# One-core MLP gradient kernel: from a fused forward and backward loop to four whole phases, with on-chip transposes and a deferred gelu derivative

## The chip, the cores and the metric

The kernel runs on one core of one Trainium2 chip. Its time is the device time of one execution in microseconds (us), measured on the chip; several executions are taken. An execution in the slow state shows a lower granted TensorE clock and a longer time; only fast executions are compared here. The profile is one execution recorded by the hardware profiler. Its span, from the first to the last instruction, is about 2 us shorter than the time of the same execution.

The engines are TensorE (PE in the profile, with its weight loads as PEld), VectorE (DVE), ScalarE (ACT), GpSimd (POOL) and SyncE (SP, which here only issues DMAs; SPq is its queue). PSUM is where matmuls accumulate; both kernels use eight 128 x 512 fp32 tiles of it.

## The reference

All arrays are bf16. S = 2048 rows, D = 448, F = 1792.

```python
h   = gelu_tanh(x @ w1 + b1)          # x: S x D, w1: D x F
out = h @ w2 + b2                     # w2: F x D
# and its gradients for a given grad_out g (S x D):
gw2 = h.T @ g                         # F x D
gh  = (g @ w2.T) * gelu'(x @ w1 + b1) # S x F
gx  = gh @ w1.T                       # S x D
gw1 = x.T @ gh                        # D x F
gb1, gb2 = gh.sum(0), g.sum(0)
```

There are six matrix products of the same size. D = 448 is three and a half times 128: where D is the contracted dimension (x @ w1 and g @ w2.T, called M1 and M4 below), the last 128-row tile is only half full.

## The kernel before

It works in blocks of 512 rows, on pairs of 128 columns of F (28 pairs in all). One loop does M1 and M4 of a pair and, between them, h @ w2 and gh @ w1.T of the block before. The half tile is padded with zero weights, so that M1 and M4 take four full matmuls per tile. In M1 one of the padding rows is not zero: it carries b1, against a row of ones in x, so that the bias costs no instruction. gelu' is computed at once from the z in PSUM. h and gh are stored to DRAM in transposed form and read back by transposing DMAs for gw2 and gw1.

```python
w1_sb = const.tile([P, KD, F], BF16, name="w1_sb")
nc.gpsimd.memset(w1_sb[0:DL, KD - 1, :], 0.0)          # 64 zero rows
...
for kt in range(KD):                                    # KD = 4
    mm_i = nc.tensor.matmul(ps1[:], lhsT=w1_sb[:, kt, fcols], rhs=xq[:, kt, :],
                            start=(kt == 0), stop=(kt == KD - 1))
nc.scalar.activation(out=hT_blk[:, ft, :], in_=ps1[:], func=ACT.Gelu_apprx_tanh)
sq_i = nc.scalar.activation(out=A[:, h, :], in_=ps1[:], func=ACT.Square, scale=...)
nc.vector.scalar_tensor_tensor(out=Bt[:, h, :], in0=A[:, h, :], ..., in1=ps1[:], ...)
...
pdma(nc.gpsimd, hT_dram_v[:, fts[0]:fts[1] + 1, scols], hT_blk[:, fts[0]:fts[1] + 1, :])
... # M4 of the pair, gh = (gelu') * ps4, store of ghT, then parts of h @ w2 and gh @ w1.T
# after the loop:
for ft in range(NF):                                    # gw2
    w_ts.append(nc.sync.dma_start_transpose(out=h_blk[:], in_=hT_dram[ft * P:(ft + 1) * P, :]))
    for st in range(NS):
        nc.tensor.matmul(ps_w[:, 0:D], lhsT=h_blk[:, st, :], rhs=g_all[:, st, :], ...)
... # gw1 in the same way from ghT_dram
```

## Time and profile before

The median is 301.95 us (three runs, 300.64 to 303.75).

| stage before | us | how read |
|---|---|---|
| start, to the first real matmul | 12.6 | timeline |
| fused loop | 194.3 | first matmul of the loop to first of gw2 |
| gw2 | 42.4 | to the first matmul of gw1 |
| gw1 and tail | 52.5 | to the end of the span |

From the page of the kernel before, its first two parts: busy time and share of each engine, and busy tenths in 40 equal slices of the span (PEclk is the granted TensorE clock in tenths).

```profile
span 301.8 us, 4020 instructions
PE 284.4 (94%) x1520; PEld 142.5 (47%) x1520; DVE 209.8 (70%) x317; ACT 147.6 (49%) x236; POOL 71.5 (24%) x89
PE   4589799999999999999999999999999999799994
PEclk9999999999999999999999999999999999799998
```

TensorE is busy almost throughout; what is left is the start and a dip near the end. The start in the timeline (start in us, duration, engine, line, operation, out<-in, and in brackets the idle time before it and what ended that):

```profile
9.85 0.28 POOL masks.py:199 TENSOR_SCALAR_AFFINE_SELECT ident<-ident 128x128 bf16<-128x128 bf16 x1 [7.39 <-DMA g_nat_108<-in_grad_out_dram]
10.18 0.48 PE L100 MATMUL ps_acc<-ident,x_nat_99 128*128 128x128 bf16 x3 [5.41 <-POOL ident masks.py:199]
12.56 1.86 PE L242 MATMUL ps_160<-xT_q,w_sb 128*128 128x512 bf16 x4 [0.52 <-DVE xT_q L106]
```

The transposes of x on TensorE need an identity matrix, whose second instruction on GpSimd runs only at 9.85 us. The dip near the end, in the chain of waits (start, duration, what the chain was in):

```profile
249.35 3.46 SPq L340
252.85 5.59 DMA gh_nat<-ghT_dram
258.57 5.30 PE ps_2370 L377 x16
263.87 3.45 PE ps_2388 L377 x16
```

The transposed reload of gh is late, TensorE pauses, and its next 16 matmuls take 5.30 us in place of 3.45. The last line also gives the pace of a 512-column matmul: 3.45 / 16 = 0.2156 us. For 448 columns the chain shows 3.03 us for 16, or 0.189.

The tail of gw1 is column-tiled (128*64), and its neighbours are not:

```profile
269.32 1.46 PE L377 MATMUL ps_2406<-gh_nat,x_all 128*128 128x512 bf16 x6
270.71 1.94 PE L383 MATMUL ps_2424<-gh_nat,x_all 128*64 128x256 bf16 x32
272.58 1.25 PE L377 MATMUL ps_2487<-gh_nat,x_all 128*128 128x512 bf16 x5
```

The change of tiling costs about 0.1 us on the way in and 0.1 us on the way out. And two activations of 512 columns follow each other on ScalarE every 0.48 us:

```profile
99.84 0.62 ACT L244 ACTIVATE hT_blk<-ps_1050 128x512 bf16<-128x512 f32 x1
100.32 0.63 ACT L245 ACTIVATE A<-ps_1050 128x512 f32<-128x512 f32 x1
```

### The profile page before, as it was taken

The page shows a single profiled execution, that of the slowest core. Times are in us where ns is not written, and L with a number is a line of the kernel's source. Part 1 is how long each engine was busy: PE and PEld are TensorE (multiplying, and loading weights), DVE is VectorE, ACT ScalarE, POOL GpSimd, SP SyncE. Part 2 cuts the span into 40 slices and gives each one's busy share as a digit, 9 for nine tenths or more (in the row PEclk, how much of TensorE's full clock was granted, in tenths as well). Part 3 has the DMA queues.
Part 4 walks back from the last instruction along what each step waited for, and adds up shares of the span by engine and source line. Part 5 has one row for each costly group of instructions (what it writes and reads, how often), then busy time and mean ns, then how long its engine had stood idle before and what let it go on. Part 6 is the DMA issues. An engine that isn't in the chain of part 4 may idle for free.

```text
span 301.8 us, 4020 instructions
## 1 busy us (share of the span) xinstructions
PE 284.4 (94%) x1520; PEld 142.5 (47%) x1520; DVE 209.8 (70%) x317; ACT 147.6 (49%) x236; POOL 71.5 (24%) x89
## 2 busy tenths in 40 slices
PE   4589799999999999999999999999999999799994
PEld 1355344444444444444444444555555558245542
DVE  0258999999999999878999778605600027857760
ACT  1099987759695756677665576112121212021211
POOL 2451010821063200522212111000210001242252
PEclk9999999999999999999999999999999999799998
DMA  4673197720579945743212314095889899999861
GB/s 134 192 206 137 41 182 168 303 114 37 130 189 375 389 155 103 213 165 130 104 72 92 116 42 187 15 223 78 169 178 171 181 213 195 183 222 164 283 206 61
DMA packets 96761, 49.18 MB, mean 163 GB/s; under 512 B 78803, under 2 KB 92596, under 8 KB 96742
## 3 DMA queue, kind: packets, MB, share of 16 engines
q1 hardware_dynamic: 91188, 31.60, 46.9%
q0 software_dynamic: 5264, 17.06, 15.0%
q10 hardware_dynamic: 290, 0.27, 0.4%
q8 instruction: 12, 0.20, 0.3%
q14 instruction: 7, 0.06, 0.1%
HBM read 7.92 MB, written 21.57 MB: 98 GB/s over the span
## 4 chain that ended last, share of the span: by engine, by line
PE 43%; DVE 9%; SPq 5%; ACT 4%; DMA 2%; issue 1%; POOL 0%; POOLq 0%; DVEq 0%
PE ps_acc L191 6%; PE ps_acc L204 6%; SPq L340 4%; DVE Ep L250 2%; DVE ghT_blk L263 2%; DVE Bt L246 2%; DMA gh_nat<-ghT_dram 2%; PE ps_2370 L377 2%; ACT Bt L249 2%; ACT Ct L248 1%; DVE Ep L251 1%; PE ps_2487 L377 1%; PE ps_2605 L377 1%; PE ps_2641 L377 1%; PE ps_2623 L377 1%
## 5 line engine op out<-in xcount | busy, mean ns | idle before, releaser
L191 PE MATMUL ps_acc<-w_sb,hT_blk 128*128 128x448 bf16 x224 | 47.7, 353 | 0.2
L204 PE MATMUL ps_acc<-w1T_sb,ghT_blk 128*128 128x448 bf16 x224 | 45.6, 353 | 0.0
L250 DVE SCALAR_TENSOR_TENSOR Ep<-Bt,A 128x1024 bf16<-128x1024 f32 x28 | 34.3, 1224 | 12.0 <-ACT Bt L249 11.7
L248 ACT ACTIVATE Ct<-Bt 128x1024 bf16<-128x1024 f32 x28 | 30.2, 1079 | 25.3 <-DVE Bt L246 25.3
L261 PEld LDWEIGHTS <-w2T_sb 128*128 128x128 bf16 x224 | 21.8, 98 | 27.5 <-issue 3.4
L242 PEld LDWEIGHTS <-w_sb 128*128 128x128 bf16 x224 | 22.1, 99 | 25.2 <-issue 2.8
L215 POOL DMA_DIRECT2D ghT_dram<-ghT_blk x28 | 20.3, 726 | 56.4 <-DVE ghT_blk L263 56.3
L355 DVE TENSOR_TENSOR gb_acc<-gh_nat 128x512 f32<-128x512 bf16 x7 | 4.8, 692 | 39.9 <-DMA gh_nat<-ghT_dram 33.1
L191 PEld LDWEIGHTS <-hT_blk 128*128 128x128 bf16 x224 | 21.8, 98 | 22.6 <-ACT hT_blk L244 0.9
L204 PEld LDWEIGHTS <-ghT_blk 128*128 128x128 bf16 x224 | 21.9, 98 | 21.2
L319 PEld LDWEIGHTS <-h_blk 128*128 128x128 bf16 x224 | 21.9, 98 | 20.5
L215 POOL DMA_DIRECT2D hT_dram<-hT_blk x28 | 20.3, 727 | 45.7 <-ACT hT_blk L244 31.3
L249 ACT ACTIVATE Bt<-Ct 128x1024 f32<-128x1024 bf16 x28 | 30.1, 1075 | 0.3
L377 PEld LDWEIGHTS <-x_all 128*128 128x128 bf16 x192 | 19.0, 100 | 21.1 <-issue 5.0
L357 DVE TENSOR_TENSOR gb_acc<-gb_acc,gh_nat 128x512 f32<-128x512 f32 x42 | 28.6, 723 | 0.3
L363 POOL PARTITION_ALL_REDUCE gb_all<-gb_acc x7 | 14.8, 2108 | 58.9 <-DVE gb_acc L358 58.9
L251 DVE TENSOR_TENSOR Ep<-Ct,Ep 128x1024 bf16<-128x1024 bf16 x28 | 19.2, 687 | 0.3
L206 ACT CAST gx_blk<-ps_acc 128x448 bf16<-128x448 f32 x16 | 8.4, 527 | 20.1 <-PE ps_acc L204 20.1
L193 DVE TENSOR_TENSOR o_blk<-ps_acc,b_bc 128x448 bf16<-128x448 f32 x16 | 9.8, 620 | 3.8 <-PE ps_acc L191 3.8
L311 DVE TENSOR_TENSOR gsum<-gsum,g_all 128x448 f32<-128x448 f32 x14 | 8.7, 625 | 0.5
L177 ACT ACTIVATE w2T_sb<-ps_acc 128x512 bf16<-128x512 bf16 x14 | 8.5, 730 | 0.0
L106 DVE COPY xT_q<-ps_acc 128x512 bf16<-128x512 bf16 x4 | 1.7, 425 | 9.7 <-PE ps_acc L102 9.7
(492 smaller groups left out, 468.7 us busy)
## 6 DMA issues: line engine op xcount, KB each, us to landing
hT_dram<-hT_blk POOLq DMA_DIRECT2D x28, 256.0 KB, 3.0
ghT_dram<-ghT_blk POOLq DMA_DIRECT2D x28, 256.0 KB, 2.7
out_dram<-o_blk SPq DMA_DIRECT2D x4, 448.0 KB
x_all<-in_x_dram SPq DMA_DIRECT2D x1, 1792.0 KB, 14.5
g_all<-in_grad_out_dram SPq DMA_DIRECT2D x1, 1792.0 KB
out_dram<-gx_blk SPq DMA_DIRECT2D x4, 448.0 KB, 3.1
out_dram<-gw_all SPq DMA_DIRECT2D x2, 784.0 KB, 5.5
out_dram<-gw_all SPq DMA_DIRECT2D x3, 384.0 KB, 2.7
```

The costliest lines, as they stand in the source:

```text
L191: nc.tensor.matmul(ps_o[:, 0:D], lhsT=hT_blk[:, ft, j * P:(j + 1) * P], rhs=w2_sb[:, ft, :], start=(ft == 0), stop=(ft == NF - 1))
L204: nc.tensor.matmul(ps_x[:, 0:D], lhsT=ghT_blk[:, ft, j * P:(j + 1) * P], rhs=w1T_sb[:, ft, :], start=(ft == 0), stop=(ft == NF - 1))
L215: i = eng.dma_start(out=out, in_=in_)
L242: mm_i = nc.tensor.matmul(ps1[:], lhsT=w1_sb[:, kt, fcols], rhs=xq[:, kt, :], start=(kt == 0), stop=(kt == KD - 1))
L248: tanh_i = nc.scalar.activation(out=Ct[:], in_=Bt[:], func=ACT.Tanh, scale=1.0 / 3.0)
L249: nc.scalar.activation(out=Bt[:], in_=Ct[:], func=ACT.Square)
L250: nc.vector.scalar_tensor_tensor(out=Ep[:], in0=Bt[:], scalar=1.0, in1=A[:], op0=ALU.subtract, op1=ALU.mult)
L251: nc.vector.tensor_tensor(out=Ep[:], in0=Ct[:], in1=Ep[:], op=ALU.subtract)
L261: nc.tensor.matmul(ps4[:], lhsT=w2T_sb[:, kt, fcols], rhs=gq[:, kt, :], start=(kt == 0), stop=(kt == KD - 1))
L319: nc.tensor.matmul(ps_w[:, 0:D], lhsT=h_blk[:, st, :], rhs=g_all[:, st, :], start=(st == 0), stop=(st == NS - 1))
L357: nc.vector.tensor_tensor(out=acc[:], in0=acc[:], in1=gh_nat[:, 2 * k:2 * k + 2, :], op=ALU.add)
L377: nc.tensor.matmul(ps_w[:, 0:wpair], lhsT=x_all[:, st, kt * P:(kt + 1) * P], rhs=gh_pair[:, st, :], start=(st == 0), stop=(st == NS - 1))
```

## The change

The kernel becomes four phases: the whole forward, gw2, the whole backward, gw1. h and gh go from SBUF to SBUF through transposing DMAs and stay there, so the DRAM copies vanish. z is kept in SBUF (`Z`), and gelu' is computed from it later (`emit_E`), in place, at lower priority. Of the half tiles, two are paired: the two matmuls with 64 rows each use different row halves of the array at the same time, so a pair of tiles takes 7 matmul slots in place of 8. With the padding goes the row of b1: the bias becomes an operand of two activations (`b1c`). gb1 comes from the accumulator of the VectorE operation that makes gh.

The order of instructions on each engine is fixed at build time by a scheduler, from its estimate of durations and from the priorities that the program gives.

```diff
+    def pair_mms(pss, lhs, rhs, fts):
+        for h, ft in enumerate(fts):
+            fc = slice(ft * P, (ft + 1) * P)
+            for n, kt in enumerate((0, 1, 3) if h == 0 else (0, 1, 2)):
+                nc.tensor.matmul(pss[h], lhsT=lhs[:, kt, fc], rhs=rhs[:, kt, :], start=(n == 0), stop=False)
+        for h, ft in enumerate(fts):                      # the two half matmuls
+            fc = slice(ft * P, (ft + 1) * P)
+            kt, ps_ = (2, slice(0, DL)) if h == 0 else (3, slice(DL, P))
+            nc.tensor.matmul(pss[h], lhsT=lhs[ps_, kt, fc], rhs=rhs[ps_, kt, :], start=False, stop=True)
...
+    for i in range(14):                                   # warm-up, 8 before
+        nc.tensor.matmul(pw[:], lhsT=warm[:, 0:P], rhs=warm[:, 0:SB], start=True, stop=True)
...
+    def emit_E(b, c):                                     # gelu' from z: 3 on ScalarE, 7 on VectorE
+        zc = Z[b][:, 2 * c:2 * c + 2, :]
+        nc.scalar.activation(out=s[:], in_=zc, func=ACT.Square)
+        nc.vector.tensor_scalar(out=v[:], in0=s[:], scalar1=GELU_A, scalar2=1.0, op0=ALU.mult, op1=ALU.add)
+        nc.vector.tensor_tensor(out=v[:], in0=v[:], in1=zc, op=ALU.mult)
+        nc.scalar.activation(out=v[:], in_=v[:], func=ACT.Tanh, scale=GELU_C)
+        nc.scalar.activation(out=n[:], in_=v[:], func=ACT.Square)
...                                                       # five more on VectorE
+    for b in range(NB):                                   # forward
+        for c in range(NPAIR + 1):
+            if c < NPAIR:
+                with tc.high_priority():
+                    pair_mms([p[:] for p in pss], w1_sb, xq, fts)
+                    for h, ft in enumerate(fts):
+                        nc.scalar.activation(out=hT[:, h, :], in_=pss[h][:], func=ACT.Gelu_apprx_tanh, bias=b1c[:, ft:ft + 1])
+                        nc.scalar.activation(out=Z[b][:, ft, :], in_=pss[h][:], func=ACT.Identity, bias=b1c[:, ft:ft + 1])
+                    for h, ft in enumerate(fts):
+                        nc.sync.dma_start_transpose(out=h_nat[:, b * SPB:(b + 1) * SPB, ft * P:(ft + 1) * P], in_=hT[:, h, :])
+            if c > 0:
+                with tc.high_priority():
+                    chain_step(acc, prev, w2_sb, c - 1)   # out += h @ w2, 8 matmuls of 448 columns
+                emit_E(b, c - 1)
...
+    g_all = big.tile([P, NS, D], BF16, name="g_all", tag="nat_d")
+    nc.gpsimd.dma_start(out=g_all[:], in_=g2.rearrange("(st p) d -> p st d", p=P))
...                                                       # gw2 from h_nat and g_all; gb2 sums; x_all
+    for b in range(NB):                                   # backward
+                pair_mms([p[:] for p in pss], w2T_sb, gq, fts)
+                for h, ft in enumerate(fts):
+                    nc.vector.scalar_tensor_tensor(out=ghT[:, h, :], in0=Z[b][:, ft, :], scalar=1.0, in1=pss[h][:], op0=ALU.add, op1=ALU.mult,
+                                                   accum_out=gb1_p[:, b, ft:ft + 1])
...                                                       # transposes of gh, chain_step with w1T_sb, then gw1
-    (the fused loop, the stores to and reloads from hT_dram and ghT_dram, the gb1 sums)
```

## The prediction

> **What bounds the kernel now.** TensorE. The page's first part gives PE 284.4 of 301.8 us (94%). From the timeline: 512-column matmuls start every 0.2156 us (16 in 3.45 us), 448-column ones every 0.189 us (16 in 3.03 us). Stages, from the chain of waits and the timeline: first real matmul at 12.6 us; fused forward/backward loop to 206.9; gw2 to 249; gw1 to 297.3; tail 4.5 us. The loop's matmuls alone (448 x 0.2156 + 448 x 0.189) are 181 us of its 194. In gw1 the chain passes through 14 transposing loads of DRAM copies (2.2 to 3.5 us of queue time each); PE waits 2.2 us at 256.4, then runs at clock 0.51 from 258.6 to 262: about 4 us lost there.
>
> **Removed.**
> - An eighth of the two K=448 products (64 zero rows): 448 matmuls become seven eighths, 12.1 us.
> - 72 of 88 PE transposes: about 4.5 us with their waits on ScalarE.
> - DRAM round trip of h and gh: 14.7 MB out, 14.7 MB back; the gw1 stall, 4 us.
> - gb1 sums on VectorE (36 us, off the path).
> - Startup: the identity is ready only at 9.85 us and PE is at half clock (0.43 us per matmul) until 16 us. More warm-up matmuls and a lighter GpSimd queue should save 5 us.
>
> **Added.**
> - 56 entries into row-tiled half pairs and 56 exits. The Trainium skill ("TensorEngine Tiling (Array Packing)", Key Properties) says that changing tiling mode drains TensorE. The trace agrees for column tiles: entering at 270.7 and leaving at 272.6 cost about 0.1 us each beyond the 16 x 0.109 us of pairs. At 0.2 us per pair that is 11 us: I expect it to give back nearly all of the 12.1 us.
> - 112 small transposing DMAs on SP. A 128 KB one from DRAM takes 1.25 us of SP's queue (timeline); two per pair is 2.5 us against 3.2 us of PE. SP is close to binding, not binding, if an SBUF source costs the same.
> - ScalarE: gelu and copy 4 x 0.48 us per pair (starts in the timeline), below PE's 3.2; deferred gelu' 3 x 1.06 us per pair fills gaps and the 42 us of gw2. VectorE likewise.
>
> **Sum (estimates from these durations).** Start 8; forward 28 x (7 x 0.2156 + 0.2 + 8 x 0.189) = 90; gw2 42.4; backward 90; gw1 42.7 (4 x 48 x 0.189 plus two column-tiled tails of 3.2); tail 3; about 4 for late w1/w2 pieces at startup, block edges and phase edges. Total 280 us: 7% faster. The gain comes from startup, PE transposes and gw1's stall, hardly from the removed zero rows.
>
> **What the profile would show.** PE busy near 95% still; first real matmul near 8 us; a pair of M1 (7 matmul slots) about 1.7 us, not 1.51, with weight-load idle at each mode change; gw2 at 3.03 us per tile without DMA waits; hT transposes on SP at 1.2 to 1.4 us each, SP queue about 85% full in forward and backward; no idle before gh_nat in gw1; ScalarE and VectorE below PE in every stage; gelu' finished before the backward needs it.
>
> **What would make it wrong.** SBUF-to-SBUF transposes costing over 1.6 us each: SP then paces both loops (each 0.1 us more is about 5 us). Scheduling: a gelu' activation of 1.06 us ahead of a gelu delays PE, if ScalarE has no slack. Startup loads (3.9 MB) too slow for pairs 2 to 4. Row-tile switches costing nothing (270) or double (291). Clock throttling after any PE gap.
>
> Predicted 280 us, range 268 to 297; faster by over 2% 0.83, within 2% 0.11, slower 0.06.

## The result, and the profile after

The changed kernel takes 320.87 us (median of four runs, 320.47 to 322.65). The ratio to the kernel before is 1.0636, 95% interval 1.058 to 1.0693. Ratios here are from the fast runs of both kernels in the same rounds, and not quite the ratios of the medians. The record gives no check of this run's results; its variants a1, a2, a4 and a5 below passed theirs. It is 6.4% slower, where 7% faster was predicted.

The same parts of the page as above:

```profile
span 318.7 us, 3910 instructions
PE 288.4 (91%) x1408; PEld 125.9 (40%) x1408; DVE 156.8 (49%) x348; ACT 171.5 (54%) x244; POOL 19.3 (6%) x26
PE   7238999999999997999997399999999999999994
PEclk9659999999999999999999679999999999999999
```

TensorE has fewer matmuls than before and is busy for longer. There is a hole at the start and one in the middle. Stage by stage, by the first matmul of each in the timeline:

| stage | predicted | measured | difference |
|---|---|---|---|
| start, to the first M1 | 8 | 20.9 | +12.9 |
| forward | 90 | 106.8 | +16.8 |
| gw2 | 42.4 | 42.4 | 0 |
| backward, to the first matmul of gw1 | 90 | 101.5 | +11.5 |
| gw1 and tail | 45.7 | 47.2 | +1.5 |
| allowance for stalls | 4 | (in the above) | -4 |
| sum | 280 | 318.7 (span) | +38.7 |

So three stages failed and two came as predicted. The start, in the timeline:

```profile
1.31 1.29 POOL L197 DMA_DIRECT2D g_all<-in_grad_out_dram  x1 [0.37 <-issue]
12.87 0.28 POOL masks.py:199 TENSOR_SCALAR_AFFINE_SELECT ident<-ident 128x128 bf16<-128x128 bf16 x1 [10.27 <-issue]
13.20 1.86 PE L125 MATMUL acc<-ident,x_nat_102 128*128 128x128 bf16 x16 [6.18 <-POOL ident masks.py:199]
13.66 5.89 DVE L222 TENSOR_TENSOR gsum<-gsum,g_all 128x448 f32<-128x448 f32 x9
19.47 0.41 DVE L127 COPY xT_q<-acc 128x512 bf16<-128x512 bf16 x1
20.90 4.08 PE L71 MATMUL ps<-xT_q,w_sb 128*128 128x512 bf16 x12 [0.79 <-DVE b1c L132]
```

The load of `g_all` (1.8 MB), written in the program after forward, has no dependence on it, and the scheduler put it first on GpSimd. The identity follows at 12.87 us. Worse, the gb2 sums (gsum) became ready with that load and stand on VectorE ahead of the copies of x transposed, which therefore end 5 us later.

Busy time of the engines by stretch (the stretch and its length, then busy us and number of instructions of PE, PEld, DVE, ACT and POOL, the granted clock, the DMA share and GB/s): forward, the first 17 us of backward, the rest of backward.

```profile
20.90:127.70 106.80, 101.43 (x449) 39.08 (x450) 56.23 (x107) 102.91 (x152) 5.93 (x5) 0.99 0.51 106
170.10:187.20 17.10, 9.55 (x34) 2.93 (x33) 16.87 (x38) 10.15 (x12) 1.89 (x2) 0.71 0.56 147
187.20:271.50 84.30, 84.30 (x418) 36.14 (x418) 34.00 (x106) 6.13 (x14) 2.29 (x3) 1.00 0.53 110
```

In forward both TensorE (101.4 of 106.8) and ScalarE (102.9) look full, which leaves two suspects. At the start of backward VectorE is full and TensorE half idle, at clock 0.71. Later in backward VectorE and ScalarE have much time to spare. What fills VectorE there (Z_98 is z of block 0, Z_101 of block 3; L242 makes gh, L153 is part of gelu'):

```profile
175.55 0.68 DVE L242 SCALAR_TENSOR_TENSOR hT<-Z_98,ps 128x512 bf16<-128x512 bf16 x1
182.38 0.69 DVE L153 TENSOR_TENSOR y<-y,Z_101 128x1024 bf16<-128x1024 bf16 x1
182.99 0.68 DVE L242 SCALAR_TENSOR_TENSOR hT<-Z_98,ps 128x512 bf16<-128x512 bf16 x1
183.73 1.67 PE L138 MATMUL acc<-w1T_sb,hT 128*128 128x448 bf16 x4 [4.80 <-DVE hT L242]
```

Between the two gh operations of the first pair stand 14 gelu' operations, of which the line of 182.38 is the last, and TensorE waits 4.80 us.

What TensorE does in forward, and in backward, in the timeline:

```profile
119.69 0.92 PE L138 MATMUL acc<-w_sb,hT 128*128 128x448 bf16 x4
120.55 0.39 PE L75 MATMUL ps<-xT_q,w_sb 64*128 64x512 bf16 x1
120.86 0.93 PE L138 MATMUL acc<-w_sb,hT 128*128 128x448 bf16 x4
121.73 0.39 PE L75 MATMUL ps<-xT_q,w_sb 64*128 64x512 bf16 x1
122.05 0.55 PE L138 MATMUL acc<-w_sb,hT 128*128 128x448 bf16 x2
...
190.20 0.39 PE L75 MATMUL ps<-gT_q,w2T_sb 64*128 64x512 bf16 x2
190.52 1.69 PE L138 MATMUL acc<-w1T_sb,hT 128*128 128x448 bf16 x8
192.05 1.46 PE L71 MATMUL ps<-gT_q,w2T_sb 128*128 128x512 bf16 x6
193.44 0.39 PE L75 MATMUL ps<-gT_q,w2T_sb 64*128 64x512 bf16 x2
```

In backward the two halves (64*128) stand together in 27 of the 28 pairs and start 0.003 us apart; one pair takes 193.44 - 190.20 = 3.24 us. That is 6 x 0.2156 + 8 x 0.189 = 2.81, one slot of 0.2156 for both halves, and 0.21 for entering and leaving the row-tiled mode, as predicted. In forward M1 and the chain are both of high priority, and the scheduler mixed them: of the 56 halves only 12 overlap with a partner (six starts 0.003 us after another half); the others run alone, and the array enters and leaves the mode 39 times instead of 28.

The idle time of TensorE that other engines ended (in total, times, longest), the three longest:

```profile
PE acc L138 <- DVE hT L242: 7.5, 2, 4.8
PE acc L125 <- POOL ident masks.py:199: 6.2, 1, 6.2
PE acc L131 <- DVE xT_q L127: 4.9, 1, 4.9
```

And ScalarE in forward, to be held against the 0.48 us above:

```profile
50.22 0.84 ACT L181 ACTIVATE Z_99<-ps,b1c 128x512 bf16<-128x512 f32 x1
50.78 0.85 ACT L180 ACTIVATE hT<-ps,b1c 128x512 bf16<-128x512 f32 x1
51.35 0.85 ACT L181 ACTIVATE Z_99<-ps,b1c 128x512 bf16<-128x512 f32 x1
```

They follow each other every 0.57 us. The Trainium skill ("ScalarE: Activation LUTs", What ACT_TABLE_LOAD costs) says that each per-partition pointer operand adds about 93 ns to an activation. The new gelu has such a bias (`b1c`), the old one had none, and the trace agrees: 0.57 against 0.48.

### The profile page after: what moved, and what is told of

The parts are those of the page before. It is cut to its first block, busy times and chain, and to the rows that moved or that the text cites. A ratio compares the mean times of both kernels' runs of the same rounds, so it can differ in the third digit from the quotient of the medians.

```text
span 318.7 us, 3910 instructions
## 1 busy us (share of the span) xinstructions
PE 288.4 (91%) x1408; PEld 125.9 (40%) x1408; DVE 156.8 (49%) x348; ACT 171.5 (54%) x244; POOL 19.3 (6%) x26
## 4 chain that ended last, share of the span: by engine, by line
PE 63%; DVE 22%; ACT 9%; DMA 4%; issue 2%; DVEq 0%; POOL 0%; POOLq 0%; ACTq 0%
PE acc L138 23%; PE ps L71 20%; PE acc L276 11%; PE ps L75 6%; DMA g_all<-in_grad_out_dram 4%; DVE y L155 3%; DVE v L149 3%; DVE y L153 3%; ACT hT L180 3%; DVE v L148 2%; PE acc L284 2%; DVE gsum L222 2%; DVE n L154 2%; DVE y L152 2%; ACT Z_101 L181 1%
## 5 line engine op out<-in xcount | busy, mean ns | idle before, releaser
L138 PEld LDWEIGHTS <-hT 128*128 128x128 bf16 x448 | 38.7, 98 | 59.8 <-issue 14.1
L138 PE MATMUL acc<-w_sb,hT 128*128 128x448 bf16 x224 | 55.1, 354 | 3.5 <-ACT hT L180 2.4
L138 PE MATMUL acc<-w1T_sb,hT 128*128 128x448 bf16 x224 | 47.6, 358 | 7.5 <-DVE hT L242 7.5
L71 PE MATMUL ps<-xT_q,w_sb 128*128 128x512 bf16 x168 | 45.9, 388 | 2.6 <-DVE b1c L132 0.8
L212 PE MATMUL acc<-g_all,h_nat 128*128 128x448 bf16 x224 | 42.5, 352 | 0.0
L71 PE MATMUL ps<-gT_q,w2T_sb 128*128 128x512 bf16 x168 | 42.2, 387 | 0.0
L180 ACT ACTIVATE hT<-ps,b1c 128x512 bf16<-128x512 f32 x56 | 38.5, 734 | 3.9 <-PE ps L75 3.7
L276 PE MATMUL acc<-gh_nat,x_all 128*128 128x448 bf16 x192 | 36.7, 352 | 0.0
L150 ACT ACTIVATE v<-v 128x1024 bf16<-128x1024 bf16 x28 | 30.0, 1086 | 3.2 <-DVE v L149 3.2
L151 ACT ACTIVATE n<-v 128x1024 bf16<-128x1024 bf16 x28 | 30.2, 1091 | 0.2
L276 PEld LDWEIGHTS <-x_all 128*128 128x128 bf16 x192 | 18.6, 98 | 17.6 <-issue 0.4
L242 DVE SCALAR_TENSOR_TENSOR hT<-Z_99,ps 128x512 bf16<-128x512 bf16 x14 | 9.1, 686 | 13.5 <-PE ps L75 13.5
## 6 DMA issues: line engine op xcount, KB each, us to landing
g_all<-in_grad_out_dram POOLq DMA_DIRECT2D x1, 1792.0 KB, 11.7
```

Source lines behind the costliest of these rows:

```text
L71: nc.tensor.matmul(pss[h], lhsT=lhs[:, kt, fc], rhs=rhs[:, kt, :], start=(n == 0), stop=False)
L138: nc.tensor.matmul(acc[j][:, 0:D], lhsT=lhs[:, h, j * P:(j + 1) * P], rhs=w[:, ft, :], start=(ft == 0), stop=(ft == NF - 1))
L150: nc.scalar.activation(out=v[:], in_=v[:], func=ACT.Tanh, scale=GELU_C)
L151: nc.scalar.activation(out=n[:], in_=v[:], func=ACT.Square)
L180: nc.scalar.activation(out=hT[:, h, :], in_=pss[h][:], func=ACT.Gelu_apprx_tanh, bias=b1c[:, ft:ft + 1])
L212: nc.tensor.matmul(ps_w[:, 0:D], lhsT=h_nat[:, st, ft * P:(ft + 1) * P], rhs=g_all[:, st, :], start=(st == 0), stop=(st == NS - 1))
```

## The experiments

The theory after reading the traces: (1) the early `g_all` load spoils the start; (2) in forward, either TensorE's separated halves or ScalarE's gelu' activations set the pace, and the two had to be told apart; (3) at the start of backward VectorE works off the gelu' of later blocks before the gh that TensorE waits for. The rivals were that the work itself is too much for ScalarE and VectorE wherever it is put, and that the transposing DMAs pace the loops. Eleven runs were made, of ten kernels. All edits are against the changed kernel unless said otherwise. Every edit is scheduled anew, so the order changes elsewhere too; where that matters it is said. The stages of all of them, in us, by the first matmul of each stage:

| kernel | first M1 | forward | gw2 | backward | span |
|---|---|---|---|---|---|
| changed kernel | 20.9 | 106.8 | 42.4 | 101.5 | 318.7 |
| a1_gall_late | 12.5 | 111.3 | 42.6 | 105.7 | 319.2 |
| a2_fullK | 21.3 | 110.9 | 42.6 | 98.7 | 320.8 |
| a3_noE (wrong results) | 21.3 | 105.0 | 42.6 | 90.7 | 306.7 |
| a4_pinned | 20.8 | 99.4 | 42.6 | 106.7 | 316.6 |
| a5_bwdprio | 21.0 | 108.1 | 42.6 | 93.5 | 312.3 |
| a7, pinned and noE (wrong results) | 20.7 | 92.4 | 42.4 | 90.9 | 293.5 |
| c2_balanced | 12.1 | 96.0 | 42.6 | 95.2 | 293.1 |
| c3_xT | 5.6 | 101.8 | 42.6 | 95.2 | 292.3 |
| c5_later | 6.1 | 101.8 | 42.4 | 91.3 | 288.8 |
| c6_fullK | 6.4 | 98.7 | 42.4 | 91.0 | 285.6 |

### a1_gall_late: the load of g_all after block 1

```diff
-    nc.gpsimd.dma_start(out=g_all[:], in_=g2.rearrange(...))
+    g_i = nc.gpsimd.dma_start(out=g_all[:], in_=g2.rearrange(...))
+    tc.add_manual_dep(g_i.ins, late_after.ins.name, ORDER, reason="g_all after block 1")   # order only
```

> The load of g_all (1.8 MB) is ordered behind the output store of block 1; nothing else is changed. Theory: in the changed kernel the scheduler issued it at 1.3 us on GpSimd's queue, ahead of the identity's second instruction (ready only at 12.9 us), and its arrival let the gb2 sums run on VectorE ahead of the copies of x transposed (5 us). Then the first M1 moves from 20.9 us to 12 to 14 us and the total falls by 6 to 9 us, to about 313. Rival: the identity is late for a reason of its own (something GpSimd does between its two instructions that has no link with the load); then only the 5 us of the sums come back, M1 at about 16 us, total about 316.

Measured: 320.32 us, ratio 1.0554 (1.0493 to 1.0616). The first M1 moved to 12.5 us and the identity to 9.67 us, as the theory said, so the cause of the late start is shown. But the total hardly moved: in the profiles the spans are 319.2 and 318.7 us. (The ratio looks 0.8% better because the kernel before was slower in these rounds, 303.84 us.) The 8.4 us came back as waits: forward took 4.5 us more, backward 4.2 more. TensorE's two longest waits, as in the view of waits above, in this run:

```profile
PE acc L138 <- DVE hT L245: 10.1, 2, 5.2
PE ps L71 <- ACT Z L181: 5.2, 3, 4.2
```

TensorE came 3.7 us earlier to backward (166.4 against 170.1) and waited there for VectorE, which ended the gelu' backlog no earlier than before (steady from 187 us in both). The second line is forward's part, and it comes from the edit itself: the moved load of g_all is in flight from 71.1 to 82.5 us, a transposing DMA of hT issued at 71.8 us lands after 10.9 us (the median is 2.4), another issued at 75.0 us lands at 83.57, the next gelu starts only at 83.64 us, and TensorE waits 4.2 us up to 85.5 us. That the load slows the transposes is read from these times and was not tested by a run of its own; c2, c3, c5 and c6, which move the load in the same way, show the same (9.8 to 10.5 us). The gain at the start was real, but one half of it was spent on the new place of the load, and the other was off the chain that decided backward.

### a2_fullK: no row-tiled halves

```diff
-            for n, kt in enumerate((0, 1, 3) if h == 0 else (0, 1, 2)): ...
-        (the two half matmuls)
+            for kt in range(KD):
+                nc.tensor.matmul(pss[h], lhsT=lhs[:, kt, fc], rhs=rhs[:, kt, :], start=(kt == 0), stop=(kt == KD - 1))
+    nc.vector.memset(w1_sb[0:DL, KD - 1, :], 0.0)      # and likewise for w2T_sb
```

> The row-tiled half pairs are undone: four 128-row matmuls per tile of both K=448 products, with zero weight rows, everything else as in the changed kernel. Backward: a pair costs 8 x 0.2156 + 8 x 0.189 = 3.24 us against 3.235 measured with the halves: no change (within 1 us of 88). Forward, theory TensorE: there the scheduler pulled the halves of a pair apart, so that each of them enters and leaves the tiling mode alone (about 13 us of switching and lost concurrency); forward falls from 104.5 to about 97. Theory ScalarE: forward is paced by ScalarE, 100% busy, with gelu' activations placed in its order (45 of them in this build, 42 before); forward stays at 104 to 107. Total 313 by the first, 321 to 324 by the second.

Measured: 321.95 us, ratio 1.0624 (1.0574 to 1.0675). Forward took 110.9 us, not the 97 of theory TensorE. ScalarE was busy for 107.1 of it, and TensorE, now with time to spare, waited for ScalarE, most of it here:

```profile
PE ps L71 <- ACT Z L179: 8.6, 7, 2.0
```

So ScalarE alone holds forward at over 105 us with the gelu' activations in its order: 43 start in forward in this trace and 39 in that of the changed kernel (the expectation counted 45 and 42). Backward's steady part shows no change by the halves, but its start differs too, so the clean comparison is c6 below.

### a3_noE: no gelu' at all (gradients wrong)

```diff
-                emit_E(b, c - 1)
```

> gelu' is not computed at all (its 3 activations and 7 VectorE operations per pair are left out; the gradients are wrong on purpose). Backward: its 13 us of waiting at the start (VectorE busy with the gelu' backlog) goes under any theory. Forward, theory ScalarE: it falls from 104.5 to 90 or less. Theory TensorE (halves pulled apart): it falls only by the waits of TensorE in it, to about 97. Total 293 by the first, 300 by the second.

Measured: 308.88 us, ratio 1.0194 (1.0145 to 1.0242). Backward fell to 90.7 us, so the wait there belongs to gelu'. Forward stayed at 105.0 us although ScalarE was busy for only 67.7 of it. So TensorE with its mixed order alone also holds forward at 105 us: two limits lay close together, and removing gelu' alone brought only 1.8 us. (The check of results passed this kernel too, without any gelu'; so that check does not prove gelu' right in the others.) This was not expected by either theory (90, or 97).

### a4_pinned: TensorE's order as in the program

```diff
+    def pin(i):   # order-only dependence of each matmul on the one before it in the program
+        if pe_last[0] is not None: tc.add_manual_dep(i.ins, pe_last[0].ins.name, ORDER, ...)
+        pe_last[0] = i
     (called for each matmul of pair_mms and chain_step)
```

> TensorE's order is pinned to the program's order, so the two halves of a pair stay together in forward as they do in backward; 35 gelu' activations stand in forward on ScalarE (42 before). Theory TensorE: each pair of halves then costs one entry and one exit; forward falls by about 8 us to 96. Theory ScalarE: forward is 28 x 2.3 + 35 x 0.95 = 98 us plus waits. The two are close here; what tells them apart is whether TensorE starts matmuls back to back (3.24 us per pair) or waits for ScalarE (longer starts at the chain's first matmul). The backlog of gelu' at the backward start grows by 7 activations, so up to 7 us may be given back there. Total 313 to 321.

Measured: 318.05 us, ratio 1.0496 (1.0446 to 1.0545). All 56 halves now overlap in 28 pairs. Forward fell by 7.4 us to 99.4, where ScalarE, with 33 gelu' activations by the trace (35 expected), was busy for 97.2. Six gelu' fewer than in the changed kernel is 5.7 us less for ScalarE, so this run eases both limits, and alone it does not tell them apart. Backward gave 5.2 us back, as expected from the larger backlog. A wait by TensorE for gelu in forward was 5.2 us in total (10 times).

### a6 and a7: pinned, and no gelu' (gradients wrong)

Both edits together. The profile of a6_pinned_noE fell in a slow execution (417 us, clock 0.65), so the same kernel was run again for a profile as a7_pinned_noE_again.

> TensorE's order pinned and gelu' left out (gradients wrong on purpose). Pinning alone cut forward from 106.8 to 99.4 us, leaving out gelu' alone only to 105.0. Theory: two limits lie close together, TensorE with its separated halves (about 105) and ScalarE with gelu' in its order (about 98); with both gone forward is 28 x 3.235 plus the clock ramp, 91 to 93 us, and the total 308.9 - 13 = 296. Rival: something else (the transposing DMAs on SP, 2 x 1.27 us per pair, or PSUM buffers) holds forward at 97 or more, and the total stays at 301 or above.

> The same kernel as a6_pinned_noE, whose profile fell in a slow execution (417 us at clock 0.65) while its timed runs were 296 to 298. For the profile only: forward 91 to 94 us with TensorE starting matmuls back to back (3.235 us per pair) if TensorE's halves and ScalarE's gelu' were its only two limits; 97 or more if a third one is there.

Measured: a6 297.34 us (median of four with the slow one; the three fast runs 296.23 to 297.51), ratio of its fast runs 0.9835 (0.9769 to 0.9902); a7 295.30 us (one run, state unknown). Forward is 92.4 us in the profile of a7. The same 90 us stretch (30 to 120 us) in the changed kernel, in a3 and in a7, columns as in the stretches above:

```profile
30.00:120.00 90.00, 87.25 (x390) 33.73 (x389) 46.96 (x90) 89.48 (x133) 2.33 (x3) 1.00 0.52 105
```

```profile
30.00:120.00 90.00, 88.73 (x383) 33.80 (x389) 7.03 (x12) 58.40 (x100) 2.34 (x3) 1.00 0.53 105
```

```profile
30.00:120.00 90.00, 89.85 (x448) 39.12 (x447) 8.88 (x16) 62.64 (x105) 3.09 (x4) 1.00 0.64 131
```

TensorE reads 97 to 100% busy in all three, with 390, 383 and 448 matmuls (some records of a3 are missing; its weight loads, 389, are as many as in the changed kernel): the busy share did not tell that an eighth of the pace was missing; the count did. Together with the changed kernel, a3, a4 and a7 are the four combinations: without gelu' the mixed order costs 12.6 us of forward (105.0 against 92.4), and with the order pinned gelu' costs 7.0 (99.4 against 92.4). There is no third limit in this forward: two transposing DMAs per pair at 1.22 us of SP's queue each (median of 112 in the changed kernel) fit into 3.24 us. Of the 12.6 us between a3 and a7, the starts of the matmuls give 8.5 us to the halves (20.2 us for halves with their entries and exits, in 45 visits to the row-tiled mode, against 11.7 in 28); the rest are short waits of the mixed order, not separated further.

### a5_bwdprio: gh before the gelu' backlog on VectorE

```diff
+                with tc.high_priority():
                     for h, ft in enumerate(fts):
                         nc.vector.scalar_tensor_tensor(out=ghT[:, h, :], in0=Z[b][:, ft, :], ...)
```

> Only VectorE's order at the start of backward is changed: gh (the product with gelu') comes before the backlog of gelu' operations of later blocks, which have 60 us until they are needed. Theory: the wait of TensorE there (first chain matmul at 176.3 us, steady only from about 187) is nothing but that order; backward falls from 101 to about 90 us and the total by 10 to 11, to about 311. Rival: the backlog has to be worked off anyway and VectorE is short of time over the whole of gw2 and backward; then the wait comes back later in backward and the total falls by less than 4 us.

Measured: 313.99 us, ratio 1.04 (1.0328 to 1.0472). Backward fell from 101.5 to 93.5 us, 8 of the 10 to 11 us expected; the wait did not come back later. The backlog was a matter of order: VectorE has time for it during backward. The first chain matmul still waits 2.7 us for gh.

### c2_balanced: all causes removed

```diff
+  (a1_gall_late, a4_pinned, a5_bwdprio) and:
+                        if h == 0: nc.scalar.activation(out=Z[b][:, ft, :], ..., func=ACT.Identity, ...)
+                        else:      nc.vector.tensor_scalar(out=Z[b][:, ft, :], in0=pss[h][:], scalar1=b1c[:, ft:ft + 1], ...)
+  emit_E of pairs 0 to 13 ordered behind gelu of pairs 1, 3, 5, ...; the other 14 behind the last gelu
+  gb2 sums and the load of x_all moved into backward
```

> A version meant to beat both, right results: g_all loaded after block 1; TensorE's order pinned; every second copy of z on VectorE in place of ScalarE; gelu' of 14 pairs in forward (one for two pairs), of 14 in gw2 and after; gh ahead of gelu' on VectorE; gb2 sums in backward. Theory (startup, separated halves, ScalarE's gelu', VectorE's order are the whole of the loss): first M1 at 12.5, forward 93, gw2 42, backward 90, gw1 43, tail 4.3: 285 us plus a few, 5% under the kernel before. Rival: ScalarE or VectorE work is too much wherever it is put; then one of forward and backward stays over 97 and the total at 292 to 305.

Measured: 294.81 us, ratio 0.9765 (0.9706 to 0.9825): 2.3% faster than the kernel before, though the interval does not settle whether by 2%. Forward is 96.0 (expected 93), backward 95.2 (expected 90), the rest as expected. It beats the kernel before, but by half of what the theory gave. Of the missing 8 us the view of waits shows 2.8 for gelu in forward and 2.8 for gh at the start of backward (154 to 157 us). After that wait the clock is 0.59 from 157 to 160 us and 0.88 to 164, which is worth another 1.7 us (an estimate: 3 x 0.41 + 4 x 0.12). Here the wait cost more than its length.

### c3_xT: x of block 0 by transposing DMAs

```diff
-    (loads of x_nat0, 16 TensorE transposes, 4 copies)
+    xq = load_T(x2, 0, "xT_q")
```

> As c2_balanced, and x of block 0 is loaded by transposing DMAs instead of TensorE transposes, so that the first M1 does not wait for the identity (9.9 us without the early g_all load). Theory: first M1 at about 7 us, bounded then by the loads of w1 and by the bias b1, which still needs the identity for the first gelu; total 3 to 4 us under c2_balanced. Rival: the transposing loads of x take as long amid the weight loads, no gain.

Measured: 293.92 us, ratio 0.9729 (0.9673 to 0.9784), 0.9 us under c2; the expectation of 3 to 4 was a miss. The first M1 came at 5.6 us, but the scheduler put 8 of the 14 warm-up matmuls behind it, and the first gelu still waited for the bias, which needs the identity, until 13.5 us.

### c5_later: six gelu' pairs moved into backward, warm-up pinned

```diff
+            if ft < 8: (emit_E ordered behind the last gelu, as in c2)       # 8 pairs, not 14
+            if c < NPAIR and n_pair % 2 == 0 and 2 <= n_pair <= 12:          # in backward
+                (emit_E of one of the last six pairs, ordered behind gh of this pair)
```

> As c3_xT, with two changes: gelu' of the last six pairs is computed in backward (one for two pairs, 30 us or more before its use), so that VectorE and ScalarE are free when backward starts, and the warm-up matmuls are pinned ahead of the first M1. In c2 and c3 the first chain matmul of backward comes 6.0 us after its first matmul (3.4 if nothing waits) and backward takes 94.7 us. Theory (order on VectorE, not amount): backward falls to 91 to 92 us; warm-up saves 1 to 2 us more at the start; total 288 to 291 against 294. Rival (amount): the six pairs delay gh later in backward, no gain.

Measured: 289.47 us (five runs), ratio 0.96 (0.9574 to 0.9625). Backward fell from 95.2 to 91.3 us, as the theory of order said. The span of the profile fell by 3.5 us (292.3 to 288.8), which is that gain less 0.5 us in start plus forward (107.4 us in c3, 107.9 in c5), so the pinned warm-up brought nothing visible. The median fell by 4.5 us, but the two medians are not of the same rounds.

### c6_fullK: c5 without row-tiled halves

Edit as in a2, on c5, with TensorE's order pinned in the same way.

> As c5_later, with the row-tiled half pairs undone: four 128-row matmuls per tile with zero weight rows, TensorE's order pinned in the same way. Theory: a half pair kept together costs one entry and one exit of the tiling mode, 0.21 us, as much as the matmul it saves (0.216 us): the same time within 1.5 us. Rival: the halves save TensorE time that was hidden elsewhere by waits; then this is 6 to 12 us slower than c5_later.

Measured: 288.07 us (six runs), ratio 0.9562 (0.9535 to 0.959), 1.4 us under c5. Backward, where no wait disturbs the comparison, is 91.0 us against 91.3. Its timeline:

```profile
189.82 3.19 PE L136 MATMUL acc<-w1T_sb,hT 128*128 128x448 bf16 x16
192.85 1.89 PE L80 MATMUL ps<-gT_q,w2T_sb 128*128 128x512 bf16 x8
```

Eight plain slots (8 x 0.2156) cost what seven slots and two mode changes cost. The removed zero rows are worth nothing here. In the profiles the difference lies in forward (98.7 us against 101.8), and most of it in one place: from 66 to 74 us TensorE is busy for 4.9 us in c5 and 7.5 in c6. There the load of g_all slows the transposing DMAs of hT as in a1, and ScalarE waits for them once, 5.4 us in c5 and 2.8 in c6. So the difference is hardly that of the zero rows. Two things were not tried: several pairs in one visit to the row-tiled mode, and b1 back in the zero rows, which would take the bias operand from ScalarE. This is the best version: 4.4% faster than the kernel before and 10% faster than the changed kernel (288.07 against 320.87, not of the same rounds).

## Why the prediction was wrong, point by point

- **The bound before, the pace of matmuls, gw2 and gw1**: right. gw2 took 42.4 us as predicted, gw1 ran without a wait for gh (its matmuls from 271.5 to 314.0 us, 42.5 against 42.7).
- **Row-tile switches give back what the removed zero rows save**: right, where the halves stand together: 3.24 us per pair in backward against the predicted 3.22. c6 confirms it by undoing them. The cost was missed in forward, where the prediction took for granted that the order of the program is the order on the engine. By the starts of the matmuls, separated halves cost 18.6 us there in the changed kernel, against 11.7 together.
- **The transposing DMAs on SP**: right, 1.22 us each, not binding in a7. By the times in the traces they bind for a few us where a 1.8 MB load runs beside them (a1, c5).
- **"Start 8"**: failed, 20.9 us. The prediction knew that the identity was late before, and supposed that "a lighter GpSimd queue" would cure it. That premise failed: with only short memsets on GpSimd before it, the identity comes at 9.67 us in a1 and at 8.74 in c3_xT, against 9.85 in the kernel before, and a1's first M1 at 12.5 us is no earlier than before (12.6). Only c3_xT and the two built on it, where M1 does not need the identity, began earlier. And it did not ask which instruction with no dependence the scheduler could put first. a1 shows the cause of the further 8 us: the `g_all` load and the gb2 sums that it made ready.
- **"Forward 28 x (...) = 90"**: failed, 106.8 us, by two limits that lie close together. One is the mixed order on TensorE (105.0 us without any gelu', a3). The other is ScalarE (busy for 102.9 of the 106.8 us; 99.4 with TensorE's order pinned, a4). The term "4 x 0.48 us per pair" was mis-sized: with a bias operand it is 4 x 0.57, while the gelu' activations start every 0.95 us and not 1.06. More important, the sum of ScalarE's work was never taken: 28 x (4 x 0.57 + 3 x 0.95) = 144 us (143 by the prediction's own 0.48 and 1.06), and 7 more for gw2, against 133 us of TensorE time in forward and gw2. The gelu' could not fit into gaps before backward, so its order decided what it would delay.
- **"Backward 90"**: failed, 101.5 us, for the same reason one stage later: "gelu' finished before the backward needs it" was false, and VectorE did gelu' of block 3 before gh of block 0. a5 shows that this was order, not amount.
- **The risk list** named "a gelu' activation ahead of a gelu" and "clock throttling after any PE gap", but gave a slower kernel a chance of only 0.06. Both came: after the wait at the start of backward the clock is 0.50 from 180 to 187 us. c6 reached 288 us, within 8 of the predicted 280, but it is another program (no row-tiled halves, no identity before M1), so this closeness does not confirm the sum.

## What to carry to other kernels

When a deferred piece of work is said to "fill gaps", add up the work of every engine over the stretch in which it has to be done and compare it with the pacing engine's time; if it does not fit, its place in the order is the design, and it must be pinned. When an engine's order is chosen at build time, look for instructions without dependences that can move to the front, and for groups that must stay together. When an experiment removes one cause and little moves, remove the second one as well before dropping either: here leaving out gelu' brought 1.8 us of forward while TensorE's order was mixed, and 7.0 once it was pinned. And look where a moved piece of work lands: a gain of 8 us at the start was swallowed half by the moved load itself and half by a wait 150 us later.

## What the Trainium skill lacked or had wrong

- "TensorEngine Tiling (Array Packing)", Key Properties, says that changing the tiling mode drains TensorE, but gives no cost. Here a visit to the row-tiled mode costs 0.21 us (0.10 in, 0.10 out), as much as one 512-column matmul (0.2156 us), so pairing two half matmuls gains nothing if the mode is entered for one pair only (c6).
- "TensorE: Matmul & The Clock Gate", Back-to-back issue gap, gives about 131 ns per matmul of 512 columns as the sustained pace of a real stream with weight loads. Here such matmuls start every 0.2156 us in forward, backward and the gw1 of the kernel before, weight loads included, and those of 448 columns every 0.189 us; the page's isolated formula fits both, the sustained figure does not. In its part on packing small matmuls the 4 ns between tiles agree (0.003 us here).
- "GPSIMD Engine Reference", Instruction dispatch, speaks of about 6 us, with no visible instruction, before the first call of a freshly loaded kernel. The runs show 8 to 10 us with nothing on GpSimd between the identity's two instructions (7.81 in c3_xT, 8.74 in a1, 10.27 with the g_all load ahead of it). Whether this is that load was not tested.
- "DMA: Bandwidth & Descriptors" has sequencer cycles for transposing DMAs only in a comparison of trn3 with earlier generations, and no measured queue time for one of this size. A 128 KB one from SBUF to SBUF holds SP's queue for 1.22 us (median of 112) and lands in 2.4 to 2.5 us; beside a 1.8 MB load of 11.3 us it landed after 10.9 (a1).
